# Attention scores as three single-pass products of split keys and queries, on row halves of the matmul array

## The chip, the cores and the metric

The kernel runs on one core of a Trainium2 chip. The core has a matmul engine (PE; its weight loads are listed apart as PEld), a vector engine (DVE), a scalar engine (ACT), a GpSimd engine (POOL) and DMA queues, all of which run their own instruction streams and wait for each other on semaphores. The metric is the device time of one execution in microseconds, median over runs; lower is better.

## What is computed

An attention layer with pooled queries feeds two feed-forward layers. Cut to what matters:

```python
q_pool = q.reshape(B, H, S // 2, 2, D).mean(axis=3)          # B=2, H=8, S=1152, D=64
scores = scale * np.matmul(q_pool, k.transpose(0, 1, 3, 2))  # 576 queries x 1152 keys for each of 16 heads
scores = scores - np.max(scores, axis=-1, keepdims=True)
attn = np.exp(scores)
attn = attn / (np.sum(attn, axis=-1, keepdims=True) + 1e-09)
x = np.matmul(attn, v)                                       # then heads are joined: 1152 tokens x 512
h = x @ w_in;  x = softplus(h) @ w_out                       # 512 -> 2048 -> 512
h = x @ w_in2; x = (P(h) / (Q(h) + 1e-6)) @ w_out2           # a rational function of h
```

q and k are drawn with a spread of 0.8, so the scores have to be accurate to well below one.

## The kernel before, in words

All work is described to a small planner (`Plan`): each operation has an engine, a duration that the author gives it, the buffers that it reads and writes, and a priority. `Plan.order` simulates the engines by these durations and writes the instruction streams in the order that it finds; the priorities are a start time by position in the work plus an offset from the tables `OFF` and `OFF2`. Buffers have no fixed addresses: each *kind* of buffer has a list of slots in SBUF (`arena`, `arena_r`) or in the eight PSUM banks, and a buffer takes a slot that is free. Kinds of phase 1 (the feed-forward layers) can share slots with kinds of phase 0 (the attention), and get them once those are all placed and done.

The attention runs over 16 heads, each in two *units* of 288 queries. For a head:

- keys and queries come in by DMA; POOL adds pairs of queries (L428);
- PE transposes the keys (L443, nine blocks of 128 keys, packed in pairs, so that the upper 64 rows of a packed block belong to one key block and the lower 64 to another) and the queries (L455). Each of the four transposed pieces of a head goes to PSUM bank 4 (kind `tp`, one slot, which it shares with `mT`) and is copied to SBUF: two pieces by ACT (L338), two by DVE (L340), chosen by `KEV` and `QEV`;
- for each unit, `scores` (L571) multiplies: keys are the stationary operand, queries move. A *pair* of key blocks is one operation; there are four of them in a unit, and the last has the ninth key block behind it, with its 288 queries divided over both row halves (144 each). The products are plain fp32 in four 64x64 tiles of the array. The result goes to one of two slots of two banks each (kind `sc`), where DVE takes the running maximum (L484) and ACT copies it to SBUF (L338);
- the maximum over keys goes through two PE transposes (L503, L513) and a DVE reduction (L507); DVE and POOL subtract it (L597), ACT takes the exponential (L604), PE multiplies with the values and with ones (L534);
- the row sums go through DRAM, POOL normalises (L631) and splits the result in a rounded part `xh` and a rest `xl` (L342, L353).

The feed-forward layers already compute with split operands: both factors are a part rounded to `float32r` and a rest, and three products (high-high, high-low, low-high) are summed (L721 for the first matrix, L803 for the second). `L353` is the line of the helper that subtracts, `L338` that of ACT copies, whatever the operation. The planner's cost of three such products with n columns is `pe_t(3, n)`; the costs of one scores operation were 0.476 us, and 0.724 us for the last of a unit.

## Time and profile before

| | us |
|---|---|
| median of 3 runs | 691.98 (691.31 to 693.44) |
| the profiled execution | 691.12 |
| its span in the trace | 689.3 |
| PE busy | 666.6 (97%) |
| DVE / ACT / POOL busy | 543.0 / 532.4 / 518.1 |

The times are of whole executions; the span is what lies between the first and the last instruction of the profiled one, so 1.8 us lie around it. Busy PE time is modelled: a matmul counts as busy until its result has drained, so the distance between the starts of two runs of matmuls is the better measure of their cost than their listed durations. In the trace, an fp32 product shows as two records, a `float32r` product as one.

### The profile page before, as it was taken

How to read it: one execution, taken by the hardware profiler on the slowest of the kernel's cores; microseconds unless marked ns; L12 is line 12 of the kernel's file. 1: busy time of each engine (PE TensorE's matmuls, PEld its weight loads, DVE VectorE, ACT ScalarE, POOL GpSimd, SP SyncE). 2: the span in 40 equal slices, each digit the busy share in tenths (PEclk: the TensorE clock that was granted, in tenths of full speed). 3: DMA queues.
4: the chain of work that ended last, by engine and by line, in shares of the span. 5: the costliest groups of instructions: out<-in, count | busy, mean ns of one | idle time of the engine just before them, and what ended most of it. 6: DMA issues, size and time to landing. Idle time of an engine off the chain costs nothing.

```text
span 689.3 us, 15479 instructions
## 1 busy us (share of the span) xinstructions
PE 666.6 (97%) x5892; PEld 507.6 (74%) x5892; DVE 543.0 (79%) x762; ACT 532.4 (77%) x1011; POOL 518.1 (75%) x513
## 2 busy tenths in 40 slices
PE   7899999999999999999999999999999999999997
PEld 4344444444444445699999999999988989888985
DVE  4788966677777799653447889999999997788896
ACT  4678877777777788768787977788877788976763
POOL 2456857465757576997778987899997799996773
PEclk9999999999999999999999999999999999999999
DMA  7233333222222333341033577898422022201011
GB/s 220 71 86 96 79 90 81 56 64 72 69 73 55 104 123 102 103 134 58 1 94 91 162 261 266 264 315 271 128 83 71 32 62 61 78 2 46 1 47 46
DMA packets 55546, 70.92 MB, mean 103 GB/s; under 512 B 11312, under 2 KB 36912, under 8 KB 55472
## 3 DMA queue, kind: packets, MB, share of 16 engines
q1 hardware_dynamic: 55472, 69.93, 33.2%
q8 instruction: 46, 0.75, 0.5%
q14 instruction: 28, 0.23, 0.1%
HBM read 58.99 MB, written 10.78 MB: 101 GB/s over the span
## 4 chain that ended last, share of the span: by engine, by line
PE 73%; DVE 8%; POOL 6%; ACT 5%; DMA 4%; issue 4%; SPq 0%; POOLq 0%; DVEq 0%; ACTq 0%
PE banks L721 25%; PE banks L803 25%; PE banks L534 11%; PE banks L571 7%; DVE arena L484 3%; ACT arena L338 3%; PE banks L503 1%; DVE banks L785 1%; DMA arena<-in_q_dram 1%; PE banks L443 1%; PE banks L513 1%; ACT arena L604 1%; DMA rr<-arena 1%; DVE arena L597 1%; PE banks L455 1%
## 5 line engine op out<-in xcount | busy, mean ns | idle before, releaser
L803 PE MATMUL banks<-arena_r 128*128 128x384 f32 (+1 forms) x1008 | 213.4, 359 | 1.4 <-DVE arena_r L353 0.8
L721 PE MATMUL banks<-xh,arena_r 128*128 128x384 f32 x768 | 211.5, 338 | 2.5 <-DVE arena_r L353 2.3
L803 PEld LDWEIGHTS banks<-arena_r 128*128 128x128 f32 x1008 | 181.4, 188 | 16.2 <-POOL arena_r L353 1.5
L338 ACT COPY arena<-banks 128x576 f32<-128x576 f32 (+5 forms) x293 | 140.0, 523 | 55.7 <-DVE arena L484 21.9
L721 PEld LDWEIGHTS banks<-xh,arena_r 128*128 128x128 f32 x768 | 140.4, 188 | 8.9 <-DVE arena_r L353 5.9
L721 PE MATMUL banks<-xl,arena_r 128*128 128x384 f32 x384 | 129.3, 337 | 0.0
L597 POOL TENSOR_TENSOR arena<-arena 128x1152 f32<-128x1152 f32 x32 | 85.2, 2663 | 56.8 <-ACT arena L338 56.2
L785 DVE RECIPROCAL banks<-arena 128x384 f32<-128x384 f32 x48 | 122.7, 2555 | 6.6 <-POOL arena L777 5.3
L484 DVE TENSOR_TENSOR arena<-banks,arena 128x576 f32<-128x576 f32 (+1 forms) x128 | 86.7, 679 | 37.1 <-ACT arena L338 18.7
L353 POOL TENSOR_TENSOR arena<-arena 128x384 f32<-128x384 f32 x96 | 97.4, 1020 | 12.5 <-ACT arena L755 8.4
L571 PE MATMUL banks<-arena 64*64 64x288 f32 (+1 forms) x1280 | 92.3, 396 | 6.4 <-DVE arena L484 4.4
L534 PE MATMUL banks<-arena 128*32 128x288 f32 (+1 forms) x1280 | 87.5, 387 | 1.2 <-ACT arena L604 0.8
L353 POOL TENSOR_TENSOR arena_r<-arena,arena_r 128x512 fp32r<-128x512 f32 x64 | 82.3, 1296 | 7.6 <-ACT arena_r L338 7.2
L604 ACT ACTIVATE arena<-arena 128x1440 f32<-128x1440 f32 (+1 forms) x64 | 82.8, 1293 | 6.6 <-POOL arena L597 3.3
L721 PEld LDWEIGHTS banks<-xl,arena_r 128*128 128x128 f32 x384 | 72.1, 188 | 1.3
L353 DVE TENSOR_TENSOR arena_r<-banks,arena_r 128x384 fp32r<-128x384 f32 x96 | 52.9, 551 | 24.7 <-ACT arena_r L338 24.3
L571 PEld LDWEIGHTS banks<-arena 64*64 64x64 f32 x1280 | 39.2, 133 | 42.0 <-ACT arena L338 11.6
L777 POOL TENSOR_TENSOR arena<-arena 128x384 f32<-128x384 f32 x48 | 49.0, 1020 | 22.5 <-ACT arena L771 22.3
L338 ACT CAST arena_r<-banks 128x384 fp32r<-128x384 f32 x96 | 45.9, 478 | 23.0 <-DVE banks L757 13.4
L771 ACT ACTIVATE arena<-banks,par 128x384 f32<-128x384 f32 x96 | 63.6, 684 | 0.0
L534 PEld LDWEIGHTS banks<-arena 128*32 128x32 f32 x1280 | 33.7, 109 | 35.1 <-issue 11.9
L757 DVE SCALAR_TENSOR_TENSOR banks<-banks,arena 128x384 f32<-128x384 f32 x48 | 27.1, 564 | 37.0 <-POOL arena L353 36.3
(55 smaller groups left out, 927.0 us busy)
## 6 DMA issues: line engine op xcount, KB each, us to landing
arena<-in_moe_w_in_dram SPq DMA_DIRECT2D x32, 512.0 KB
arena<-in_moe_w_out_dram SPq DMA_DIRECT2D x32, 512.0 KB
sp<-arena SPq DMA_DIRECT2D x32, 256.0 KB
arena<-sp SPq DMA_DIRECT2D x32, 256.0 KB
arena<-in_k_dram SPq DMA_DIRECT2D x16, 288.0 KB
arena<-in_q_dram SPq DMA_DIRECT2D x16, 288.0 KB
arena<-in_v_dram SPq DMA_DIRECT2D x16, 288.0 KB
arena<-rr SPq DMA_DIRECT2D x16, 144.0 KB
```

The costliest lines, as they stand in the source:

```text
L338: nc.scalar.copy(o, i)
L353: e.tensor_tensor(out=o, in0=a, in1=b, op=ALU.subtract)
L484: P.op("V", dve_t(m * HW), lambda: nc.vector.tensor_tensor(out=o(), in0=x(), in1=y(), op=ALU.max), r=r, w=w, at=t0 + (OFF['mx'] + 0.15 * j ...
L534: nc.tensor.matmul(out=out()[r:r + m, o:o + w], lhsT=lhs(x, y), rhs=st()[:, x, o:o + w], start=(c == 0 and first), stop=(c == KC - 1 and l ...
L571: nc.tensor.matmul(out=ps()[y:y + D, i, o:o + w], lhsT=kx()[D * i:D * i + D, x, y:y + D], rhs=qT()[D * i:D * i + D, q0:q0 + w], start=True ...
L597: (nc.vector, nc.gpsimd)[g].tensor_tensor(out=s, in0=s, in1=mB()[:, None, :].to_broadcast([128, n, HW]), op=ALU.subtract)
L604: nc.scalar.activation(out=s, in_=s, func=AF.Exp, scale=escale)
L721: nc.tensor.matmul(out=hp(), lhsT=w()[:, kk * 128:(kk + 1) * 128], rhs=x[:, kk, :], start=(kk == 0 and n == 0), stop=(kk == KD - 1 and n = ...
L771: return lambda: nc.scalar.activation(out=o(), in_=i(), func=AF.Identity, scale=sc, bias=bi)
L777: P.op("G", pool_t(CW), lambda: nc.gpsimd.tensor_tensor(out=Q(), in0=t(), in1=ah(), op=ALU.add), r=[t, ah], w=[Q], at=a("2q"))
L785: P.op("V", (69 + 6.25 * CW) / 1e3, lambda: nc.vector.reciprocal(out=h(), in_=Q()), r=[Q], w=[h], at=a("2r"))
L803: nc.tensor.matmul(out=o()[:, 0:w_], lhsT=lt, rhs=rh, start=(f == 0 and n == 0), stop=(f == FG - 1 and n == 2),)
```

## The change

Keys and queries are split like the operands of the feed-forward layers. Each of the four transposed pieces of a head is rounded to `float32r` by ACT (`kh`, `qh`), and DVE subtracts that from the piece in PSUM (`kl`, `ql`). A pair of key blocks is then three passes (high-high, high-low, low-high); in each pass two products with 64 rows and 128 columns of the array, one for each row half, replace the four 64x64 tiles. The ninth block stays behind the fourth pair. The planner's costs of a scores operation become 0.39 and 0.68 us, and it treats them as the same kind of matmul as those of the feed-forward layers (`mode=0`). The split parts live at the end of `arena_r`, where the eighth set of weight buffers and the buffers `gh` and `gl` of the feed-forward layers lie; room that becomes free in `arena` changes the slots there, with one `raw` buffer more outside the attention's slots. All offsets of the priorities are new.

```diff
 OFF = {
-    'wait': -8.882,
+    'wait': 28.77,
...
-KEV = "AV"
-QEV = "VA"
...
-    f1 = lay(0, arena, 0, LF, ("kr", 2, 2560), ("qr", 1, 3072), ("qm", 1, 3072), ("vf", 2, 2304), ("kx", 2, 2560))
+    f0 = lay(0, arena, 0, LF, ("kr", 2, 2560), ("qr", 1, 3072), ("qm", 1, 3072), ("vf", 2, 2304))
+    f1 = f0 + 4096
     f2 = lay(0, arena, f1, LF, ("s", 4, 10368))
-    f3 = lay(0, arena, f2, LF, ("q1", 2, 2304), ("mx", 2, 1152), ("ud", 2, 2304), ("sd", 2, 1152), ("uh", 2, 1152), ("rb", 1, 2304), ("xp", 1, 2304),
+    f3 = lay(0, arena, f2, LF, ("mx", 2, 1152), ("ud", 2, 2304), ("sd", 2, 1152), ("uh", 2, 1152), ("rb", 1, 2304), ("xp", 1, 2304),
              ("mp", 2, 2304), ("mb", 2, 1152), ("mc", 2, 32), ("dc", 2, 160), ("rc", 2, 64))
+    lay(0, arena_r, LR - 20480, LR, ("kh", 2, 2560), ("kl", 2, 2560), ("qh", 2, 2304), ("ql", 2, 2304))
...
     lay(1, arena_r, 0, LR, *wch * 8, *g * 4)
-    lay(1, arena, 0, f1, ("raw", 2, 4096), ("w23", 2, 2048), ("w2", 3, 2048))
+    lay(1, arena, 0, f0, ("raw", 1, 4096), ("w23", 2, 2048), ("w2", 3, 2048))
+    lay(1, arena, f0, f1, ("raw", 1, 4096))
...
-    lay(1, arena, f3, LF, ("raw", 1, 4096), ("w23", 1, 2048))
+    lay(1, arena, f3, LF, ("raw", 1, 4096), ("w23", 1, 2048), ("raw", 1, 4096))
...
-            kx = P.buf("kx", [128, KP, 128], F32)
-            qT = P.buf("q1", [128, SQ], F32)
+            kx = [P.buf(x, [128, KP, 128], F32R) for x in ("kh", "kl")]
+            qT = [P.buf(x, [128, SQ], F32R) for x in ("qh", "ql")]
             spare = ["mB", "pv", "sm"] if first else []
+
+            def halves(t, n, src, dst, key, at):
+                hi, lo = dst
+                P.op("A", act_t(n), lambda: cp("A", hi(), src()), r=[t], w=[key[0]], at=at)
+                P.op("V", dve_t(n), lambda: sub("V", lo(), src(), hi()), r=[t, key[0]], w=[key[1]], at=at)
...
-                ee = KEV[g]
-                P.op(ee, cp_t(ee, 128 * n, True), lambda: cp(ee, kx()[:, c0:c0 + n, :], t()[:, 0:n, :]),
-                     r=[t], w=[(kx, g)], at=t0 + OFF['tke'] * T)
+                halves(t, 128 * n, lambda: t()[:, 0:n, :], [lambda x=x: x()[:, c0:c0 + n, :] for x in kx],
+                       [(x, g) for x in kx], t0 + OFF['tke'] * T)
...
-                P.op(QEV[s], cp_t(QEV[s], HW, True), lambda: cp(
-                    QEV[s], qT()[:, s * HW:(s + 1) * HW].rearrange("p (j c) -> p j c", j=3), t()),
-                    r=[t], w=[(qT, s)], at=t0 + OFF['tqe'] * T)
+                halves(t, HW, t, [lambda x=x: x()[:, s * HW:(s + 1) * HW].rearrange("p (j c) -> p j c", j=3) for x in qT],
+                       [(x, s) for x in qT], t0 + OFF['tqe'] * T)
...
-                    for y in range(0, 128, D):
+                    for n, (a, y) in enumerate(((0, 0), (0, 1), (1, 0))):
                         for i in range(2):
                             q0 = hf * HW + i * step
                             nc.tensor.matmul(
-                                out=ps()[y:y + D, i, o:o + w],
-                                lhsT=kx()[D * i:D * i + D, x, y:y + D],
-                                rhs=qT()[D * i:D * i + D, q0:q0 + w],
-                                start=True,
-                                stop=True,
+                                out=ps()[:, i, o:o + w],
+                                lhsT=kx[a]()[D * i:D * i + D, x, :],
+                                rhs=qT[y]()[D * i:D * i + D, q0:q0 + w],
+                                start=(n == 0),
+                                stop=(n == 2),
                                 skip_group_check=True,
                             )
 
-            P.op("P", 0.724 if last else 0.476, mm, r=[(qT, hf), (kx, 0), (kx, 1)] if j > 1 else [(qT, hf), (kx, 0)],
-                 w=[ps], at=at, mode=4)
+            P.op("P", 0.68 if last else 0.39, mm, r=[(x, hf) for x in qT] + [(x, g) for x in kx for g in range(1 + (j > 1))],
+                 w=[ps], at=at, mode=0)
```

## Rows read from the trace of the kernel before

**Rows 1.** Page, part 1: busy time, share of the span, instructions.
```profile
PE 666.6 (97%) x5892; PEld 507.6 (74%) x5892; DVE 543.0 (79%) x762; ACT 532.4 (77%) x1011; POOL 518.1 (75%) x513
```

**Rows 2.** Busy time by stage: window, length, each engine's busy us, PEclk, DMA, GB/s.
```profile
19.00:22.20 3.20, 0.61 (x7) 0.43 (x7) 3.08 (x4) 1.21 (x5) 2.09 (x2) 1.00 0.00 0
22.20:26.00 3.80, 3.80 (x25) 1.54 (x29) 1.19 (x4) 2.90 (x4) 2.35 (x1) 0.55 0.31 83
...
173.62:189.87 16.25, 15.82 (x236) 7.67 (x239) 11.97 (x20) 12.72 (x22) 11.48 (x12) 1.00 0.26 71
189.87:206.11 16.24, 15.81 (x235) 7.65 (x239) 11.95 (x20) 12.54 (x22) 9.11 (x8) 1.00 0.22 62
...
302.00:500.00 198.00, 197.05 (x1124) 195.84 (x1123) 149.93 (x238) 158.03 (x340) 171.82 (x188) 1.00 0.54 173
```

**Rows 3.** Chain of work that ended last, 176 to 189 us: start, us, what.
```profile
175.86 0.25 PE banks L455 x3
176.10 1.38 PE banks L571 x24
...
183.84 0.77 DVE arena L484
184.61 0.04 issue
184.65 0.72 PE banks L571 x8
...
188.28 1.13 PE banks L571 x16
```

**Rows 4.** Timeline of PE, start, us, instructions, idle time before them.
```profile
184.65 0.72 PE L571 MATMUL banks<-arena 64*64 64x288 f32 x8 [0.38 <-DVE arena L484]
```

**Rows 5.** Timeline of PE where feed-forward matmuls follow the attention's.
```profile
264.29 0.96 PE L571 MATMUL banks<-arena 64*64 64x288 f32 x16
...
266.20 0.45 PE L721 MATMUL banks<-xh,arena_r 128*128 128x384 f32 x1
266.48 0.34 PE L721 MATMUL banks<-xl,arena_r 128*128 128x384 f32 x1
...
288.30 0.79 PE L803 MATMUL banks<-arena_r 128*128 128x384 f32 x3
```

**Rows 6.** Chain, dense stretches of 384 columns (L721) and of 512 (L803).
```profile
343.27 4.17 PE banks L721 x24
...
526.52 3.40 PE banks L803 x15
```

**Rows 7.** Timeline of PE, narrow windows: the ninth block's matmuls and the ones behind.
```profile
192.81 0.42 PE L571 MATMUL banks<-arena 64*64 64x144 f32 x8
...
193.06 0.66 PE L571 MATMUL banks<-arena 64*64 64x288 f32 x8
```

**Rows 8.** Timeline of PE, the opening transposes, whose operands are float32r.
```profile
1.62 4.43 PE L653 MATMUL banks<-identr 128*128 128x128 f32 x36 [1.62 <-DVE ones L867]
5.88 0.74 PE L443 MATMUL banks<-ident,arena 128*128 128x128 f32 x5
```

**Rows 9.** Groups by shape, ACT and DVE: busy us, mean ns, idle before.
```profile
L338 ACT COPY arena<-banks 128x288 f32<-128x288 f32 x80 | 31.7, 406 | 18.1 <-PE banks L513 9.6 <-DVE arena L484 5.1 <-DVE arena L597 2.2
...
L353 DVE TENSOR_TENSOR arena_r<-banks,arena_r 128x384 fp32r<-128x384 f32 x96 | 52.9, 551 | 24.7 <-ACT arena_r L338 24.3
...
L484 DVE TENSOR_TENSOR arena<-banks,arena 128x288 f32<-128x288 f32 x32 | 14.6, 456 | 0.9
...
L340 DVE COPY arena<-banks 128x288 f32<-128x288 f32 x16 | 7.1, 445 | 1.3 <-PE banks L455 1.2
L340 DVE COPY arena<-banks 128x256 f32<-128x256 f32 x16 | 6.7, 420 | 1.9 <-PE banks L443 1.9
```

**Rows 10.** Timeline, all engines: how long pieces stand in bank 4.
```profile
175.69 0.41 PE L455 MATMUL banks<-ident,arena 96*128 96x96 f32 x3
...
176.33 0.44 DVE L340 COPY arena<-banks 128x288 f32<-128x288 f32 x1
...
177.65 0.47 PE L455 MATMUL banks<-ident,arena 96*128 96x96 f32 x3
...
179.15 0.31 PEld L443 LDWEIGHTS banks<-ident,arena 128*128 128x128 f32 x3 [0.47 <-ACT arena L338]
```

**Rows 11.** Timeline of POOL: the fifteenth of sixteen weight rests of the first layer's group.
```profile
302.71 1.31 POOL L353 TENSOR_TENSOR arena_r<-arena,arena_r 128x512 fp32r<-128x512 f32 x1
```

More of the change, by code (lines that the diff above doesn't have):

```diff
@@ L202 @@
 OFF = {
-    'wait': -8.882,
-    'slack': -1.382,
-    'ld': -812.521,
-    'tk': -11.818,
-    'tke': 1536.06,
-    'sq': -727.689,
-    'tq': -10.601,
-    'tqe': -306.514,
-    'lv': 7144.53,
-    'sc': 81.048,
-    'ev': 1752.92,
-    'mx': 906.024,
-    'mt': -1814.3,
-    'mr': 522.686,
-    'mb': -625,
-    'sh': 8796.51,
-    'ex': -150.754,
-    'stick': 770.627,
-    'ms': -5296.43,
-    'shg': -186.538,
-    'exg': 7835.02,
-    'sm': 1013.29,
-    'so': -57.276,
-    'pv': 808.435,
-    'pvs': -103.047,
-    'po': -726.257,
-    'nm': 456.872,
+    'wait': 28.77,
+    'slack': -13.759,
+    'ld': 0.198,
+    'tk': -16.966,
+    'tke': -4195.19,
+    'sq': 375.411,
+    'tq': -15.761,
+    'tqe': -260.576,
+    'lv': -1665.22,
+    'sc': 27.543,
+    'ev': 608.597,
+    'mx': 419.752,
+    'mt': -1241.4,
+    'mr': -207.398,
+    'mb': -4279.26,
+    'sh': 3841,
+    'ex': 1779.84,
+    'stick': 3184.49,
+    'ms': -2890.58,
+    'shg': -16.114,
+    'exg': 1464.57,
+    'sm': 3221.9,
+    'so': 379.479,
+    'pv': 1651.99,
+    'pvs': -414.881,
+    'po': 1120.04,
+    'nm': 315.914,
 }
 OFF2 = {
-    'ld': -118.557,
-    'hi': -1626.93,
-    'lo': 751.869,
-    'sp': -617.197,
-    'ld2': 1471.26,
-    '1a': 823.014,
-    '1d': 391.426,
-    '1y': -4944.66,
-    '1r': -1591.47,
-    '1z': -190.564,
-    '1g': 362.064,
-    'gh': 7560.96,
-    'gl': -160.245,
-    '2h': 193.884,
-    '2a': 314.78,
-    '2t': 100.782,
-    '2q': 2434.09,
-    '2b': 877.088,
-    '2A': 7670.04,
-    '2m': 2938.22,
-    '2n': -108.014,
-    '2r': 2130.37,
-    '2g': -602.386,
-    'out': 2838.23,
-    'end': 10454.9,
-    'c1': -1510.66,
-    'c2': -5603.53,
-    'co': 18.915,
-    's0': 517.435,
-    's1': 2446.21,
+    'ld': 590.296,
+    'hi': 384.693,
+    'lo': -1389.58,
+    'sp': 848.971,
+    'ld2': 286.76,
+    '1a': 587.131,
+    '1d': 1539.75,
+    '1y': -4596.15,
+    '1r': -788.05,
+    '1z': -652.263,
+    '1g': -441.645,
+    'gh': 28.699,
+    'gl': -1205.75,
+    '2h': -1678,
+    '2a': -475.889,
+    '2t': -298.715,
+    '2q': -4211.42,
+    '2b': 21.98,
+    '2A': 3258.02,
+    '2m': 1597.4,
+    '2n': 626.472,
+    '2r': 854.862,
+    '2g': -511.212,
+    'out': 5907.98,
+    'end': 4845.89,
+    'c1': -4112.39,
+    'c2': -1549.96,
+    'co': 16.991,
+    's0': 1668.77,
+    's1': 200.585,
 }
```

## The prediction

> **What bounds the kernel now.** I read the share of busy time first, then the busy time by stage, then the chain of work inside one head. PE is busy 97% of the span and no other engine passes 79% [rows 1], but that is a mean over two stages. In the feed-forward stage PE has 197.05 of 198.00 us [rows 2]: nothing there can pay but fewer matmul columns, and this change takes none. In the attention the trace repeats: from about 40 us to 265 us one head (two units) takes 16.24 us, and in two such windows PE is busy 15.8 us, ACT 12.5 to 12.7, DVE 12.0, POOL 9.1 to 11.5 [rows 2]. The chain in a head runs through PE's own order nearly everywhere. The one place where it leaves PE is a wait of 0.38 us for a scores slot that DVE's maximum still reads [rows 3, 4]. So the attention is bound by PE too, with 0.4 us of 16.24 lost to others. What PE saves in a head comes off the end as long as ACT and DVE, which the change loads, keep up.
>
> **The scores before.** A run of two pairs of key blocks takes 1.13 us; a run of two pairs and the ninth block takes 1.38 us [rows 3]. The ninth block is the difference, 0.25 us; the narrow windows agree, with its eight records between 192.81 and 193.06 [rows 7]. The planner's 0.476 a pair and 0.248 for the ninth leave 0.17 to 0.18 us for entering such a run. A unit is 4 x 0.48 + 0.24 = 2.16 us and a head 4.32, plus four entries of 0.17 us.
>
> **The scores after.** One pass is two products, one for each row half. That the halves run side by side is seen today: a pair is eight records of 288 columns in 0.48 us, 60 ns each, where a single-pass product at 2.4 GHz would stream 288 columns in 120, and the two row halves write the same partitions in different banks, as they will. For the length of a pass I take the feed-forward matmuls: 24 with 384 columns in 4.17 us, 174 ns; 15 with 512 in 3.40 us, 227 ns [rows 6]. That is 0.41 ns a column, so 288 columns take 174 - 96 x 0.41 = 135 ns. The lower bound is bare streaming, 120 ns. Three passes are 0.405 us (0.36 at least) for a pair.
>
> The ninth block has 144 columns a pass, 60 ns of streaming and 75 with the 15 ns that the rows above leave over; but each pass loads two sets of 128 weight columns. No row shows such a load alone, so it is bounded by its neighbours. The ninth block today loads 64 columns for each of its records, at 31 ns a record [rows 7], so 62 ns for 128 columns and 124 a pass, still under the 135 of a full pass. A query transpose loads 128 columns and moves 96 in 0.25 / 3 = 83 ns [rows 3]: 166 a pass. The float32r transposes at the start take (5.88 - 1.62) / 36 = 118 ns with load and stream [rows 8]: 236 a pass. The first is the nearest, because there too loads for different tiles alternate; the others hold a load and a stream that may not overlap. So the ninth costs 3 x 75 to 3 x 124, 0.23 to 0.37 us; I take 0.29, the middle. It is also what the diff's planner costs imply (0.68 - 0.39), and the old costs in that table match the trace (0.248 against 0.25).
>
> A unit is then 4 x 0.405 + 0.29 = 1.91 us, 0.25 less; a head saves 0.50. Entering a float32r run costs 0.28 - 0.17 = 0.11 us where a feed-forward run follows the attention [rows 5], against 0.17: four entries save 0.06 each, 0.25 a head. Together 0.75 us a head. Of 225 us in which PE is the bound there are 225 / 16.24 = 13.9 heads: **10.5 us off**.
>
> The Trainium skill, TensorEngine Tiling (Array Packing), Key Properties, has it that a change of tiling mode drains the engine. Row halves beside whole-array matmuls would be such a change, and the 0.25 us of entries would be gone: 7.0 us instead of 10.5. No run here shows the entry to row halves.
>
> **What is added.** In a head two pieces that DVE copied go to ACT, 288 columns at 406 ns and 256 at some 380: ACT +0.79 us. DVE loses copies of 445 and 420 ns and gains four subtractions from PSUM, 551 ns for 384 columns, 456 for each 288, some 430 for 256 [rows 9]: 1.89 - 0.87 = +1.03 us. At a head of 15.5 us ACT stands at 13.5 (87%, from 78) and DVE at 13.0 (84%, from 74). Both stay under PE. But both are in order, and behind each added instruction stand the copies and maxima that free the scores slots, for which PE already waits 0.38 us a head. From nothing to twice that 0.38 may come on top; I take 0.15 us a head, 2.1 us. In the first head one subtraction and a handover (0.46 + 0.2 us, by the same rows) lie before the first scores: 0.6 us.
>
> Bank 4 is held longer. A query piece is there from 175.69 to 176.77 and the next from 177.65 to 179.15, the last copied by ACT, with the key transposes waiting behind [rows 10]. The six holds of a head (four pieces and two maxima) are some 7 us by such rows. Each piece now waits for ACT and then DVE, so about 0.7 us more: 10 of 15.5 us. That is hidden, since pieces are made a head ahead, until waits add over 5 us.
>
> The new place of the split parts costs nothing. They end with the last scores (264.29 + 0.96 us), the first matmul that needs `gh` starts at 288.30 [rows 5], and the eighth weight set is made from 302.71 on [rows 11]. If the attention's end moved there late by 20 us it would cost; it moves earlier. The extra `raw` slot and the new offsets move work that is off the path. What they do to the few bubbles of the feed-forward stage (about 1 us each) I count as 0 with 2 us either way.
>
> **Sum.** 691.1 - 10.5 + 2.1 + 0.6 = 683.3 us for the profiled execution. The median stands 0.9 above it: **684 us**.
>
> **Rivals.**
> *The loads are the bound (slower).* A pass waits for two weight loads instead of for columns. At 83 ns a load each of the 15 passes of a unit is 166 ns, a unit 2.49 us, 0.33 more than now; 32 units give 10.6 us, less 3.5 of entries: 699 us. At 118 ns a unit is 3.54: 692 + 32 x 1.38 - 3.5 = 733 us. It decides from a pass of (2.16 + 0.12) / 15 = 152 ns, 76 ns a load. For it speaks that every row with 128 weight columns and few moving ones is above 76; against it that those rows have one tile, and the ninth block's 64 columns pass in 31.
> The Trainium skill, TensorE: Matmul & The Clock Gate, LDWEIGHTS, gives columns / 1.2 ns for a load, and so speaks against this change: an estimate by it is 107 ns a load, 214 a pass, a unit of 3.2 us and 692 + 32 x 1.05 - 3.5 = 722 us. The trace does not bear this out for loads in tiles, since 64 columns would be 53 ns there, and are 31 [rows 7].
> *ACT, DVE or bank 4 take PE's place (no change).* The saving turns into waits before the scores and key transposes: if 0.75 us a head is lost so, the head stays at 16.24 us and the time at 692. For it: DVE already ends PE's only wait. Against: both keep 2 us free a head.
> *The halves don't overlap (not what it says).* Six products of 135 ns are 0.81 us a pair, and six of 75 ns for the ninth are 0.45; a unit 3.69 us, 692 + 32 x 1.53 = 741 us. The four tiles of today speak against it.
>
> **How the numbers follow.** Forecast 0.66, loads 0.15 (most of it near 699), no change 0.12, halves 0.03, and 0.04 for a new order that is worse at several places at once, near 697. Within 0.3% (about what a measurement of this kernel can tell from no change) is 689.9 to 694.1. Faster 0.66, same 0.12, slower 0.22. The forecast's own range is 675 (passes at 120 ns and 75 for the ninth save another 0.2 us a unit, no added waits) to 690. To leave out no more than 2 in 10 the range reaches to 699.
>
> PE's clock adds a little: after the 2.6 us in which PE stands idle before 22.2 us the granted clock is 0.55 on average to 26 us [rows 2], some 1.7 us lost; a start with another gap may have that or not, and the range holds it.
>
> **What would show it.** Right: a run of two pairs near 0.81 us plus an entry of 0.1, the ninth near 0.29, a head near 15.6 us with PE still busy over 96% of it, the feed-forward stage as long as before. Wrong: a pass over 150 ns with weight loads back to back; or short passes with PE idle behind L338, L353 or L484 for over half a microsecond a head; or the head as forecast and the start or the handover to the feed-forward stage longer by several microseconds.

## The result, and the profile after

| | before | after |
|---|---|---|
| median, us | 690.15 (689.22 to 693.44, 9 runs) | 695.83 (692.88 to 696.74, 9 runs) |
| the profiled execution / its span | 691.12 / 689.3 | 695.97 / 694.2 |

After over before is 1.0068, 95% interval 1.0049 to 1.0088: the changed kernel is 0.7% slower. The forecast was 684 and "faster"; the time lies in the range (675 to 699), the direction was wrong.

The lines of the changed kernel that matter: L575 scores, L488 running maximum, L507 and L517 the maximum's transposes, L511 its reduction, L601 shift, L608 exponential, L538 values, L336 ACT's copies and roundings, L351 subtractions, L683, L686 and L689 the three DVE instructions of a weight conversion, L725 and L807 the feed-forward matrices. Each experiment below has its own numbering, a few lines off.

The page's busy times, then busy time by stage (window, length, busy us and instructions of PE, PEld, DVE, ACT, POOL, PEclk, DMA share, GB/s), against [rows 1] and [rows 2]:

```profile
PE 662.9 (95%) x5572; PEld 548.5 (79%) x5572; DVE 561.9 (81%) x794; ACT 551.2 (79%) x1043; POOL 519.8 (75%) x513
```
```profile
10.40:17.00 6.60, 5.84 (x35) 4.42 (x35) 4.84 (x9) 2.96 (x6) 0.12 (x1) 0.50 0.96 262
17.00:30.90 13.90, 12.55 (x74) 8.71 (x74) 9.55 (x16) 9.60 (x17) 7.34 (x4) 0.50 0.24 67
148.76:164.53 15.77, 15.15 (x212) 9.63 (x212) 12.79 (x21) 13.56 (x24) 9.14 (x8) 1.00 0.25 70
264.30:269.26 4.96, 0.00 (x0) 0.00 (x1) 4.78 (x9) 2.27 (x6) 4.62 (x7) 0.71 0.63 191
302.00:500.00 198.00, 196.09 (x1113) 193.74 (x1112) 148.70 (x239) 159.90 (x335) 171.02 (x186) 1.00 0.57 177
```

Three things are to be seen. The head shrank from 16.24 to 15.77 us. PE's granted clock stands at 0.50 (1.2 GHz, its lower level) for 20.5 us of the start, where before it was low for about 4 us [rows 2]; it fell behind an idle time of PE of 1.5 us, in which PE waits for keys (to 8.97). And a stretch of 5 us near the end of the attention has no matmul at all, while DVE and POOL are full. Where the 4.9 us went is read from the starts of the same work in both traces:

| start of | before | after | difference |
|---|---|---|---|
| first scores | 8.57 | 10.57 | +2.0 |
| values of unit 0 | 25.83 | 29.44 | +3.6 |
| values of unit 4 | 62.02 | 61.49 | -0.5 |
| values of unit 16 | 161.80 | 156.42 | -5.4 |
| values of unit 28 | 258.11 | 251.48 | -6.6 |
| values of unit 29 | 265.57 | 277.03 | **+11.5** |
| ninth feed-forward tile | 305.10 | 311.73 | +6.6 |
| last matmul | 685.07 | 689.94 | +4.9 |

Two neighbouring units, 28 and 29, turn a lead of 6.6 us into a lag of 11.5. Some of that comes back at once, because PE does feed-forward tiles meanwhile; 13 us are gone by the ninth tile. PE's timeline there (start, us, instructions, idle time before and what ended it), where [rows 5] has the same place of before; first, from before, the values of units 28 and 29:

```profile
258.11 1.18 PE L534 MATMUL banks<-arena 128*32 128x288 f32 x16 [0.52 <-ACT arena L604]
...
265.57 0.69 PE L534 MATMUL banks<-arena 128*32 128x288 f32 x8
```
```profile
251.48 0.69 PE L538 MATMUL banks<-arena 128*32 128x288 f32 x8
...
261.72 0.34 PE L725 MATMUL banks<-xh,arena_r 128*128 128x384 f32 x1
269.26 0.88 PE L507 MATMUL banks<-ident,arena 128*96 128x128 f32 x3 [7.20 <-DVE arena L689]
269.79 2.27 PE L807 MATMUL banks<-arena_r 128*128 128x384 f32 x6
271.85 0.52 PE L725 MATMUL banks<-xh,arena_r 128*128 128x384 f32 x1
...
277.03 2.39 PE L538 MATMUL banks<-arena 128*32 128x288 f32 x40
...
283.00 0.45 PE L725 MATMUL banks<-xh,arena_r 128*128 128x384 f32 x1 [1.94 <-DVE arena_r L351]
```

And what DVE did meanwhile, from its timeline:

```profile
261.90 0.46 DVE L488 TENSOR_TENSOR arena<-banks,arena 128x288 f32<-128x288 f32 x1
262.28 0.68 DVE L683 TENSOR_SCALAR banks<-arena 128x512 int32<-128x512 int32 x1
263.00 0.70 DVE L686 SCALAR_TENSOR_TENSOR banks<-arena,banks 128x512 int32<-128x512 int32 x1
263.73 0.69 DVE L689 SCALAR_TENSOR_TENSOR arena<-arena,banks 128x512 int32<-128x512 int32 x1
...
268.53 0.68 DVE L689 SCALAR_TENSOR_TENSOR arena<-arena,banks 128x512 int32<-128x512 int32 x1
```

Between a unit's last maximum (261.90) and the transposes that need it (269.26) DVE makes three weight conversions, 9 x 0.70 = 6.3 us. Their buffer `cv` lies in bank 4, where L507 has to write, so PE waits for the last L689. PE's clock adds to the loss. Behind each of the two waits of the timeline it stands at 0.50 (the columns are as above):

```profile
269.26:273.20 3.94, 3.94 (x15) 3.82 (x16) 3.46 (x5) 1.48 (x2) 3.86 (x5) 0.50 0.51 159
283.46:286.87 3.41, 3.41 (x15) 2.97 (x18) 2.87 (x5) 3.21 (x5) 3.24 (x5) 0.50 0.43 120
```

The first six matmuls there, of 384 columns, start over 2.06 us (269.79 to 271.85), 0.34 us each, where [rows 6] have 0.174. An estimate from these rows: half of 3.94 + 3.41 us is 3.7, and with the waits of 7.2 and 1.9 us that makes 12.8 of the 13 us.

The last instructions of the sixteen conversions of the first layer start before at 11.2, 30.7, 44.1, 59.0, 70.1, 79.7, and then from 243.2 on; after at 12.3, and then all others from 256.5 on. On DVE's timeline the sixth and seventh of before, then the first and second of after:

```profile
79.67 0.67 DVE L685 SCALAR_TENSOR_TENSOR arena<-arena,banks 128x512 int32<-128x512 int32 x1
243.16 0.67 DVE L685 SCALAR_TENSOR_TENSOR arena<-arena,banks 128x512 int32<-128x512 int32 x1
```
```profile
12.35 0.69 DVE L689 SCALAR_TENSOR_TENSOR arena<-arena,banks 128x512 int32<-128x512 int32 x1
256.49 0.68 DVE L689 SCALAR_TENSOR_TENSOR arena<-arena,banks 128x512 int32<-128x512 int32 x1
```

**Five conversions that lay in the first heads now lie at the attention's end.** That is a reading of two traces; the experiments test it, and the price of the new form beside it. Nor is all of the lead a saving of the new form. Of the 6.6 us at unit 28, 4.7 are won from unit 2 to unit 12, where the changed kernel makes no conversion: before needs 83.6 us for these five heads (from 14.0 to 18.8 us each, and 16.24 only behind them), after 78.8. The conversions are not all of that: with four of them held back, in a run below, before takes 82.2.

### The profile page after: what moved, and what is told of

Its sections match the earlier page's. It is cut to its first block, busy times and chain, and to the rows that moved or that the text cites. A ratio compares the mean times of both kernels' runs of the same rounds, so it can differ in the third digit from the quotient of the medians.

```text
span 694.2 us, 14921 instructions
## 1 busy us (share of the span) xinstructions
PE 662.9 (95%) x5572; PEld 548.5 (79%) x5572; DVE 561.9 (81%) x794; ACT 551.2 (79%) x1043; POOL 519.8 (75%) x513
## 4 chain that ended last, share of the span: by engine, by line
PE 73%; DVE 11%; ACT 8%; DMA 3%; issue 2%; POOL 2%; SPq 0%; DVEq 0%; POOLq 0%; ACTq 0%
PE banks L725 25%; PE banks L807 24%; PE banks L538 10%; PE banks L575 8%; DVE arena L601 4%; ACT arena L336 4%; ACT arena L608 2%; DVE arena L488 2%; PE banks L507 2%; DVE banks L789 2%; PE banks L449 1%; DMA arena<-in_q_dram 1%; DVE arena_r L351 1%; PE banks L517 1%; DMA arena<-sp 1%
## 5 line engine op out<-in xcount | busy, mean ns | idle before, releaser
L725 PE MATMUL banks<-xh,arena_r 128*128 128x384 f32 x768 | 214.1, 341 | 5.0 <-DVE arena_r L351 4.3
L807 PE MATMUL banks<-arena_r 128*128 128x384 f32 (+1 forms) x1008 | 214.5, 360 | 0.0
L807 PEld LDWEIGHTS banks<-arena_r 128*128 128x128 f32 x1008 | 182.6, 189 | 13.8
L336 ACT COPY arena<-banks 128x576 f32<-128x576 f32 (+5 forms) x261 | 131.3, 531 | 38.2 <-DVE arena L488 14.3
L725 PEld LDWEIGHTS banks<-xh,arena_r 128*128 128x128 f32 x768 | 141.6, 189 | 11.6 <-DVE arena_r L351 8.8
L601 POOL TENSOR_TENSOR arena<-arena 128x1152 f32<-128x1152 f32 x32 | 85.3, 2665 | 73.4 <-ACT arena L336 73.4
L725 PE MATMUL banks<-xl,arena_r 128*128 128x384 f32 x384 | 130.2, 339 | 0.2 <-POOL xl L351 0.2
L351 DVE TENSOR_TENSOR arena_r<-banks,arena_r 128x384 fp32r<-128x384 f32 (+2 forms) x160 | 82.7, 517 | 47.8 <-ACT arena_r L336 46.5
L351 POOL TENSOR_TENSOR arena<-arena 128x384 f32<-128x384 f32 x96 | 97.8, 1021 | 15.7 <-ACT arena L759 10.0
L488 DVE TENSOR_TENSOR arena<-banks,arena 128x576 f32<-128x576 f32 (+1 forms) x128 | 86.5, 677 | 28.2 <-ACT arena L336 20.8
L336 ACT CAST arena_r<-banks 128x384 fp32r<-128x384 f32 (+2 forms) x160 | 72.6, 454 | 26.3 <-DVE banks L790 9.9
L538 PE MATMUL banks<-arena 128*32 128x288 f32 (+1 forms) x1280 | 83.1, 388 | 8.0 <-ACT arena L608 8.0
L575 PE MATMUL banks<-arena_r 64*128 64x288 f32 (+1 forms) x960 | 88.6, 320 | 1.9 <-ACT arena L336 0.7
L608 ACT ACTIVATE arena<-arena 128x1440 f32<-128x1440 f32 (+1 forms) x64 | 82.7, 1292 | 5.1 <-DVE arena L601 5.0
L351 POOL TENSOR_TENSOR arena_r<-arena,arena_r 128x512 fp32r<-128x512 f32 x64 | 82.6, 1299 | 4.6 <-ACT arena_r L336 4.5
L575 PEld LDWEIGHTS banks<-arena_r 64*128 64x128 f32 x960 | 69.3, 196 | 17.5 <-issue 6.2
L725 PEld LDWEIGHTS banks<-xl,arena_r 128*128 128x128 f32 x384 | 72.7, 189 | 1.6 <-POOL xl L351 0.5
L538 PEld LDWEIGHTS banks<-arena 128*32 128x32 f32 x1280 | 35.4, 109 | 40.8 <-ACT arena L608 11.0
L775 ACT ACTIVATE arena<-banks,par 128x384 f32<-128x384 f32 x96 | 61.8, 687 | 0.0
L601 DVE TENSOR_TENSOR arena<-arena,banks 128x1440 f32<-128x1440 f32 x32 | 52.7, 1646 | 1.6 <-ACT arena L336 1.0
```

The lines of the kernel that those rows point to most:

```text
L336: nc.scalar.copy(o, i)
L351: e.tensor_tensor(out=o, in0=a, in1=b, op=ALU.subtract)
L488: P.op("V", dve_t(m * HW), lambda: nc.vector.tensor_tensor(out=o(), in0=x(), in1=y(), op=ALU.max), r=r, w=w, at=t0 + (OFF['mx'] + 0.15 * j ...
L538: nc.tensor.matmul(out=out()[r:r + m, o:o + w], lhsT=lhs(x, y), rhs=st()[:, x, o:o + w], start=(c == 0 and first), stop=(c == KC - 1 and l ...
L575: nc.tensor.matmul(out=ps()[:, i, o:o + w], lhsT=kx[a]()[D * i:D * i + D, x, :], rhs=qT[y]()[D * i:D * i + D, q0:q0 + w], start=(n == 0), ...
L601: (nc.vector, nc.gpsimd)[g].tensor_tensor(out=s, in0=s, in1=mB()[:, None, :].to_broadcast([128, n, HW]), op=ALU.subtract)
```

## Experiments: the price of the new form

**The form alone, in the order of before.** Keys and queries are rounded by the copies of before; each pair is three passes on row halves, all of the rounded parts, so the rests are left out of the scores. The rounded parts lie at the end of `arena_r`. Nothing is added on ACT or DVE, and the order of all engines is that of before.

```diff
-                    for y in range(0, 128, D):
+                    for _ in range(3):
...
-                                out=ps()[y:y + D, i, o:o + w],
-                                lhsT=kx()[D * i:D * i + D, x, y:y + D],
+                                out=ps()[:, i, o:o + w],
+                                lhsT=kx()[D * i:D * i + D, x, :],
```

> The kernel before, its order and its copies unchanged, only the scores in the new form: keys and queries are rounded by the copies that there are, and a pair of key blocks is three passes on the two row halves, all three of the rounded parts (each overwrites the one before, so that the rests are left out and PE's work is that of the changed kernel). This measures the price of the form alone, without the added ACT and DVE work and without a new order. The prediction's price (0.75 us a head): head 15.5, total 679 to 682. Theory now (weight loads show at the start of each operation, the form is worth 0.13 to 0.28 us a head): head 15.95 to 16.1, total 686 to 689. Rival (loads the bound): head at or above 16.24, 690 or more.

Measured: 688.10 us (683.59 to 689.74) against 689.85, ratio 0.9959 (0.9935 to 0.9984). The figure goes with the clock: eight of the ten executions have a granted clock of 0.987 to 0.992 over their span and take 687.45 us or more, and two have 0.997 and take 683.59 and 683.84. The profiled one, 688.38, has 0.990. Busy time by stage at the start and in two heads:

```profile
18.00:30.90 12.90, 10.90 (x73) 7.67 (x69) 7.15 (x12) 7.05 (x11) 4.41 (x2) 0.52 0.17 48
170.65:186.58 15.93, 15.44 (x216) 9.22 (x212) 11.96 (x19) 12.73 (x22) 11.47 (x11) 1.00 0.25 70
186.58:202.51 15.93, 15.44 (x215) 9.22 (x211) 11.95 (x19) 12.73 (x22) 9.16 (x7) 1.00 0.25 70
```

The form is worth 16.24 - 15.93 = 0.31 us a head, not 0.75. PE's timeline shows where the rest stays, two pairs alone and two with the ninth block:

```profile
172.83 1.06 PE L572 MATMUL banks<-arena_r 64*128 64x288 f32 x12
173.82 0.53 PE L504 MATMUL banks<-ident,arena 128*96 128x128 f32 x3
...
176.76 1.39 PE L572 MATMUL banks<-arena_r 64*128 64x288 f32 x18
178.09 0.31 PE L535 MATMUL banks<-arena,ones 128*2 128x72 f32 x8
```

A run of two pairs goes from 172.83 to 173.82, 0.99 us where the prediction had 0.81 and an entry of 0.11; with the ninth it is 1.33, where it had 1.21. The single records of these runs tell why. The two halves of a pass start 2 to 9 ns apart, and passes follow each other every 0.130 us, as forecast (0.135). But the first pass of a run starts at 172.828 and the second at 173.067, 0.24 us later. The first weight load starts at 172.826 and the second at 172.934, and the first pass's records are 0.399 us long, the next ones' some 0.29: so one load of 0.108 us shows at the start of a run, and the stream of 0.13 comes on top. From the last pass to the next work it is another 0.22. So 6 x 0.13 = 0.78 us of passes make a run of 0.99. In the run with the ninth block its three passes take 0.067, 0.113 and 0.111 us, the last two the distance of their loads, and the full pass behind them 0.18 instead of 0.13: 0.34 us in all, 1.33 - 0.99.

**The changed kernel with the old products**, in its own order: four fp32 tiles of 64x64 read the rounded parts.

```diff
-                    for n, (a, y) in enumerate(((0, 0), (0, 1), (1, 0))):
+                    for y in range(0, 128, D):
...
-                                lhsT=kx[a]()[D * i:D * i + D, x, :],
+                                lhsT=kx[0]().bitcast(F32)[D * i:D * i + D, x, y:y + D],
...
```

> The changed kernel with its scores multiplied as before, in plain fp32 on four 64x64 tiles, from the rounded parts alone; splits, buffers and the order of every instruction stream are those of the changed kernel, so that only the form of the scores differs (the rests are computed and not used). The prediction's price of the form, 0.75 us a head: a steady head grows from 15.77 to 16.5 us. The price read from the two traces, 4.96 against 5.24 us of PE a head without waits: it grows by 0.3 us or less, to 15.8 to 16.1, because some of it falls into PE's wait of 0.62 us a head. Rival (the head's length is set by DVE and ACT): it stays at 15.77 within 0.05.

Measured: 695.93 us, one run, within the 692.88 to 696.74 of the changed kernel. Over ten heads (units 4 to 24) it loses 1.3 us, 0.13 a head; it had won 2.0 by unit 4. The clock is low for 6.8 us at the start, not for 20.5:

```profile
8.90:15.70 6.80, 6.05 (x41) 3.00 (x45) 5.02 (x9) 2.79 (x6) 0.00 (x0) 0.50 0.96 289
15.70:31.00 15.30, 11.44 (x141) 5.44 (x137) 11.57 (x19) 11.28 (x21) 7.46 (x4) 1.00 0.25 78
```

So of the 0.47 us by which the changed kernel's heads are shorter, 0.13 is the form's in this order. By type of work, values take 7.11 us a head instead of 7.58 (from the starts of PE's timeline), being issued in four runs instead of seven: that is the new order, since the run with the old products, in the same order, has 7.11 too.

**The changed kernel without the third pass** (the product of the keys' rests is left out; order kept).

```diff
-for n, (a, y) in enumerate(((0, 0), (0, 1), (1, 0))):
+for n, (a, y) in enumerate(((0, 0), (0, 1))):
...
-                                stop=(n == 2),
+                                stop=(n == 1),
```

> The changed kernel without the third pass of its scores (rest of the keys times rounded queries is left out); order kept. A pass is 0.13 us of a pair and 0.11 of the ninth block when loads are hidden, so PE has 2 x (4 x 0.13 + 0.11) = 1.26 us a head less to do. If PE bounds the head it shrinks from 15.77 to 14.5 us. If the chain from scores over DVE's maximum and shift and ACT's exponential to the values bounds it (PE waits 0.62 us a head there), it shrinks by what lies on that chain alone, one to two passes for each unit: 0.3 to 0.6 us, to 15.2 to 15.5, and PE's waits grow by the rest.

Measured: 686.77 us, one run. Of 1.26 us of passes a head gives back 0.5 (15.25 us), and PE's wait before the values grows from 0.62 to some 0.75 us. The chain of work in a head of the changed kernel shows what stands there (start, us, what):

```profile
158.06 0.90 PE banks L575 x12
...
159.04 0.76 DVE arena L488
...
159.82 1.67 DVE arena L601
...
162.09 0.66 ACT arena L336
...
163.17 1.31 ACT arena L608
164.48 0.04 issue
164.53 1.18 PE banks L538 x16
```

Behind the last scores lie a maximum, a shift, copies and an exponential, 5.5 us in which PE has other work for all but 0.62. Before, PE's wait was 0.38 [rows 4].

**The changed kernel without the rests' subtractions** from the third head on (the passes read old rests).

```diff
-lambda: sub("V", lo(), src(), hi()),
+(lambda: sub("V", lo(), src(), hi())) if hd < 2 else (lambda: None),
```

> The changed kernel, its order kept, without the subtractions that make the rests of keys and queries from the third head on (the passes read old rests instead): DVE has 1.9 us less to do in a head, and bank 4 comes free after ACT's rounding. Theory (a head is set by one chain of DVE's last maximum, its shift, ACT's copies and exponential, in which the subtractions have no place): the head stays within 0.1 us of 15.77, 694 to 697. Rival (the added DVE work and the longer hold of bank 4 are what keeps the head from 15.5): the head falls to 15.5 or less, 690 to 692.

Measured: 694.16 us, one run; a head is 15.55 us. That is between the two forecasts, and a single run: by it the subtractions cost 0.22 us a head, though the chain names none of them. That they stand in DVE's queue ahead of the maxima would explain it, which no run shows.

**One pass in the order of before**: scores of rounded keys and queries alone, the rests left out.

```diff
-                    for _ in range(3):
+                    for _ in range(1):
```

> The same with one pass instead of three: scores of rounded keys and queries alone, a less accurate product than either kernel's. PE has (8 x 0.26 + 2 x 0.21) = 2.5 us a head less to do. Theory (behind PE stands a chain of DVE and ACT that is nearly as long as the head; two passes instead of three gave 0.47 of 1.26 us): head 15.2 to 15.6, total 676 to 684. Rival (PE alone sets the head): head below 14, total below 662.

Measured: 679.56 us (678.38 to 680.00), ratio 0.9833 (0.9803 to 0.9863): faster than both kernels, with a less accurate product. A head is 14.89 us, shorter than expected (15.2 to 15.6) but far from what PE's 2.5 us less would make:

```profile
177.62:192.51 14.89, 13.30 (x175) 6.71 (x171) 11.86 (x19) 12.73 (x22) 9.16 (x7) 1.00 0.29 75
```
```profile
175.23 0.47 PE L572 MATMUL banks<-arena_r 64*128 64x288 f32 x4 [0.39 <-ACT arena L338]
176.56 0.40 PE L572 MATMUL banks<-arena_r 64*128 64x288 f32 x2 [0.87 <-DVE arena L485]
```

PE now waits 1.26 us a head for scores slots that ACT and DVE still read. The attention's end keeps its order, and the lead of 10.6 us at unit 28 reaches the end (12.7 at the last matmul).

## Experiments: the start

**Weight loads later**: the early weight loads but the first are held until the second head's row sums are written, since the changed kernel issues three of them from 4.09 to 5.12 us, when the loads of the first heads are issued but not all landed, and before only one (3.14).

```diff
-r=[] if l == 0 and F < 3 else [("rr", GATE)]
+r=[] if l == 0 and F == 0 and io == 0 else [("rr", 1)] if l == 0 and F < 3 else [("rr", GATE)]
```

> The changed kernel, with the two spare weight loads that it issues at 4.6 and 5.1 us (and the next at 13.1) held until the second head is normalised; the rest of the order is the same, the weights are used from 256 us on. Theory (start lost to loads): the first key and query loads share the DMA engines with these, PE stands idle between 6.5 and 11.8 us, its granted clock falls to 0.5 at 10.4 us and stays there to 30.9. With the loads held the first scores start 1 to 2 us earlier than 10.57, the clock stays up longer, and the whole is 2 to 5 us shorter than the changed kernel. Rival (the start is late because value loads go first and because the rounded and rest parts add steps): first scores within 0.5 us of 10.57, clock as before, time within 1 us of the changed kernel.

Measured: 696.60 us (695.06 to 697.20), ratio 1.0091 (1.0073 to 1.0109) to before. The first values come 1.2 us earlier, the first scores 0.6 (10.01), and the clock is low for the same 20.5 us. The loads are a small part of the late start. What no run changes is the order of the first loads: after issues two value loads first (0.74) and its keys at 1.63, before its keys at 0.74 and the values at 3.61.

**Longer warm-up**: 20 more transposes before the keys arrive, so that PE doesn't stand idle until 9.0 us.

```diff
-            for _ in range(NWARM):
+            for _ in range(NWARM + 20):
```

> The changed kernel, its order kept, with 20 more warm-up transposes (56 instead of 36, 0.13 us each, 2.7 us) so that PE has no idle time of 1.5 us before the keys' second piece arrives at 9.0 us. Theory (the start is late because PE's clock falls after that idle time and the row-half passes then run at half speed for 20 us): the granted clock stays at 1.0 past 10 us, the first values come 2 to 4 us earlier than 29.4, and the total is 2 to 4 us less than the changed kernel's, 692 to 694. Rival (the start waits for data, for ACT's rounding and DVE's subtractions; the clock costs little): first values at 28.5 or later, total 695 to 697.

Measured: 696.81 us (695.82 to 701.97), ratio 1.0105 (1.0059 to 1.0151); first values at 29.19. The theory fell, and the figures are the rival's: PE was busy for 2.73 of the 3 us to 9.0 and the clock at 0.97 in the next 3, but it was at 0.50 from 12 to 30 all the same. The idle time had only moved: in those next 3 us PE was busy for 0.99. So this run doesn't tell whether a full clock would bring the values forward. One execution speaks against a gain in the total: of the changed kernel's nine, it has a granted clock of 0.992 over its span, against 0.977 to 0.980 in the others, and takes 695.85 us, where their median is 695.83. The runs above show when the clock is low: with the order of before and only the form changed to about 31 us, with the old form in the new order to 15.7.

## Experiments: the attention's end

**Conversions spread**: in the changed kernel four of the late conversions are put into early heads, every other instruction keeps its place (their buffer lies in SBUF; some weights come out wrong, while the amount of work is the same).

```diff
+            for i, o in enumerate((v1, v2, v3)):
+                o.start = vs[3 * (n - 1) + i].start - 1e-3
...
-        for o in P.order(0.01 * OFF['slack'], 0.01 * OFF['wait'], OFF['stick']):
+        for o in spread(P.order(0.01 * OFF['slack'], 0.01 * OFF['wait'], OFF['stick'])):
```

> The changed kernel, with four of the five weight conversions that it does between 256 and 274 us (conversion 1 to 4; three DVE operations, one ACT cast, one POOL subtraction each) done one operation per unit between heads 2 and 8, in place in SBUF instead of bank 4, their loads with them; every other operation keeps its place. Theory (handover lost to DVE): the 7.2 us in which PE waits at 262 us for a maximum queued on DVE behind three conversions shrink to under 2 us, the granted clock doesn't fall there, and the kernel is 7 to 12 us shorter than the changed one, that is 684 to 689 us, also below the kernel before. Each unit with an inserted operation may cost up to 0.3 us, 4 us in all, so the gain can be 4 us smaller. Rival (the handover is slow because ACT and DVE lag with the attention's own work, now that scores come faster): PE still waits over 5 us for the last maximum, and the time is within 2 us of the changed kernel.

Measured: 697.97 us (697.06 to 698.77), ratio 1.0114 (1.0095 to 1.0132). Neither the 684 to 689 of the theory nor the wait of the rival came. The last instructions of the four now start at 45.0, 71.4, 94.9 and 120.1 us, and cost 2.2 us there (the values of unit 16 start at 158.62, not 156.42). PE transposes the last maximum at 264.43 now, but a gap stayed behind it; PE's timeline, then DVE's:

```profile
271.16 2.56 PE L810 MATMUL banks<-arena_r 128*128 128x384 f32 x6 [6.20 <-ACT arena_r L338]
```
```profile
270.03 0.56 DVE L764 SCALAR_TENSOR_TENSOR banks<-banks,arena 128x384 f32<-128x384 f32 x1 [5.65 <-POOL arena L353]
```

PE's order had been made for late weights: one tile of the first matrix, then its second matrix, which waits for the softplus chain through ACT, POOL and DVE. Nothing else was queued in front, and the last unit's reduction stood behind that chain on DVE. Taking the conversions out of an order made around them gave nothing back, so this run alone doesn't decide between the conversions and the order.

**Before with late conversions**: four of the six early conversions of the kernel before are held to the end; the planner orders the rest.

```diff
-r=[] if l == 0 and F < 3 else [("rr", GATE)]
+r=[] if l == 0 and F < 1 else [("rr", GATE)]
```

> The kernel before, with four of its six early weight conversions (the third to the sixth) held until near the end of the attention, by one condition on their loads; the planner orders the rest anew. Theory (the attention's end is bound by DVE work that has lost its place earlier): 4 x 3 instructions of 0.70 us = 8.4 us of DVE move in front of or among the last units' maxima, PE waits several us there behind them, and the time is 6 to 12 us above the kernel before, 697 to 702, with the steady heads unchanged at 16.2 us. Rival (DVE has time left at 79% busy, so conversions can run anywhere): within 2 us of the kernel before.

Measured: 704.68 us (704.34 to 705.61), ratio 1.0206 (1.0172 to 1.0240), 13.7 us slower. About 3 us are lost in the first heads, whose order also changed; the steady heads are as before (the lag is 3.0 at unit 16 and 2.8 at unit 28). The lag is 2.8 at the first feed-forward tile and 15.0 at the ninth. PE's longest wait there ends with POOL, which subtracts for the weights' rests (from 310.0 us, in that wait, to 316.8 the granted clock is 0.50):

```profile
305.67 2.01 PE L803 MATMUL banks<-arena_r 128*128 128x384 f32 x10 [0.66 <-POOL arena_r L353]
311.78 1.01 PE L721 MATMUL banks<-xh,arena_r 128*128 128x384 f32 x2 [3.76 <-POOL arena_r L353]
```

So late conversions cost about as much (12.2 us, from a lag of 2.8 to one of 15.0) in a kernel that has none of the change's other parts, though the order that the planner finds around them is new here too. The expectation had the sign, a size somewhat too small (6 to 12 us) and the wrong place: not the last units' maxima waited here, but the tiles, for weights.

**Attention first**: the changed kernel with all operations of the attention ranked ahead of the feed-forward layers.

```diff
-M0 = -225.024
+M0 = 30000.0
```

> The changed kernel with every operation of the attention ranked ahead of every one of the feed-forward layers (one constant). Theory (the same DVE work has to fit in before the eighth tile, whatever comes first): the last units lose their hole of 7.2 us and finish about 10 us earlier, but the feed-forward tiles then wait for weights, and the total is no better than 2 us under the changed kernel: 694 to 704. Rival (the order alone is at fault: work of the feed-forward stage was put in front of the last units): the 7.2 and 1.9 us of waiting vanish and nothing takes their place, 686 to 689.

Measured: 704.48 us (702.40 to 705.12), ratio 1.0195 (1.0163 to 1.0228), half a microsecond above the top of the theory. The values of unit 29 start at 260.19 instead of 277.03, so the hole is gone; and the ninth tile starts at 322.83 instead of 311.73. The wait moved:

```profile
301.45 1.01 PE L725 MATMUL banks<-xh,arena_r 128*128 128x384 f32 x2 [4.94 <-POOL arena_r L351]
```

With the conversions late, putting the attention first is worse by 8.7 us. Other orders were not tried, so this doesn't show that the changed kernel's is the best.

**Fewer conversions**: five of the sixteen are left out of the changed kernel (the first set's weights stand in), the loads of the others held two heads later, and the order computed anew.

```diff
+            if 1 <= 2 * F + io <= 5:
+                W[0, F, io] = W[0, 0, 0]
+                return
...
-GATE = 11
+GATE = 13
```

> The changed kernel without five of its sixteen weight conversions (the second to the sixth: their loads, 15 instructions of DVE, five each of ACT and POOL; the tiles use the first set's weights in their place), the loads of the others held two heads later, and the order computed anew. It leaves out as much conversion work as the kernel before does early, in the shade of its first heads. Theory (that work, come late, is what eats the gain): 15 x 0.70 = 10.5 us of DVE vanish from the attention's end, the wait of 7.2 us with them, and the 6 to 7 us that the heads save reach the end: 684 to 689. Rival (the hole is of the new order or of the split parts' place, whatever is converted): 693 to 697.

Measured: 689.67 us (688.71 to 691.90), ratio 0.9987 (0.9966 to 1.0009) to before, 6.2 us under the changed kernel, 0.7 above what was expected. The values of unit 29 start at 265.26, level with before, and the hole of 7.2 us is closed. But one long wait stays, and again it is POOL's:

```profile
306.36 0.87 PE L728 MATMUL banks<-xh,arena_r 128*128 128x384 f32 x2 [3.60 <-POOL arena_r L351]
```

Without the five conversions, and in the new order that goes with it, about half of the 13 us is back. It comes late: at the ninth tile (309.59) this run is 2.1 us ahead of the changed kernel, at the 21st 7.2. The other eleven, whose loads were held longer here, still keep POOL behind. How much of the rest belongs to that later loading and how much to the order of the changed kernel isn't separated.

Why the changed kernel's planner puts no conversion into its heads stays open. Bank 4, which a conversion needs for 2.1 us, is held longer there, by each piece until ACT and then DVE have read it. But the new offsets also rank the conversions otherwise. By the diff `c1` goes from -1510.66 to -4112.39 (in steps of 3.95 us, counted off from `M0`) and `mx` from 906.024 to 419.752 (in steps of 7.4 us), and of what can start the smaller rank goes first: conversions at 5742 stood ahead of maxima at 6704, and at 16019 they stand behind maxima at 3106. No run tries the one without the other.

## Why the prediction was wrong, point by point

- **"PE is the bound of a head, 0.4 us of 16.24 lost to others": half right.** PE was busy throughout, yet a chain through DVE and ACT is close behind. Two passes instead of three gave 0.5 of 1.26 us, one pass in the order of before 1.35 (16.24 to 14.89) of some 2.8, which is 2.5 for the two passes and 0.31 for the form. And the head of 16.24 us doesn't hold from 40 us on: the five heads from unit 2 to unit 12 take 16.7 on average.
- **"0.75 us a head from the scores": the term was mis-sized.** A pass was right (0.13, forecast 0.135), the ninth block's own passes too (0.067 + 0.113 + 0.111 = 0.29, forecast 0.29), though the pass behind them takes 0.05 more. The entries were wrong. I took 0.11 us for entering a run, less than the 0.17 of the fp32 tiles, from feed-forward matmuls [rows 5]; measured it is 0.99 - 0.78 = 0.21, because a weight load of 0.108 us shows at the start of the run. So the 0.25 us a head of entries are gone, as in the prediction's 7.0 us; whether a drain has a part in that no run shows. The form is worth 0.31 us a head in the order of before and 0.13 in the new one.
- **"At 31 ns for 64 columns": a misreading of [rows 7].** Those records belong to four tiles, which load side by side: in the trace of before the four loads start 6 to 7 ns apart (192.812 to 192.831) and the next four 0.12 us behind the first. They say nothing of one load. The Trainium skill, TensorE: Matmul & The Clock Gate, LDWEIGHTS, has columns / 1.2, 107 ns for 128 columns. I set that aside; the traces of the new form agree with it (0.108 to 0.109 us from a first load to the next). The Trainium skill, TensorEngine Tiling (Array Packing), Key Properties, says that tiles load weights in parallel, and the loads of the two halves start 3 to 4 ns apart. Read together the two sections give an estimate of 3 x 107 ns = 0.32 us for the ninth block, against 0.34 measured, and they would have warned me off the 31 ns. The estimate by the first section beside the rival "loads the bound" had the right price for a load and the wrong sum, since it counted two loads one behind the other.
- **"0.15 us a head for ACT and DVE": about right.** The subtractions cost 0.22, by one run; no run takes out ACT's added copies.
- **"First head 0.6 us": wrong in size, and nearly without effect.** First values came 3.6 us late, but at unit 4 the changed kernel was level. The new form itself costs about 2 us there: the run with the old products is 2.0 us ahead of the changed kernel at unit 4, and the run with the new form in the order of before is 2.1 us behind that kernel at unit 10; in both pairs the granted clock at the start differs.
- **"The extra `raw` slot and the new offsets ... 0 with 2 us either way": the step that failed.** By unit 28 the lead was 6.6 us, somewhat less than the 7.8 of the forecast (10.5 less 2.1 and 0.6), and for other reasons. The 13 us lost behind it were in no term: five conversions moved from the heads to the handover, where PE waited 7.2 and 1.9 us. Whether "bank 4's longer hold is hidden" failed with it is open. The prediction looked for trouble at the handover in the new place of the split parts and in `gh`, and not in the conversions of the early heads, which cost little there (2.2 us for four, by the run that spread them). The rival with a worse order (697, chance 0.04) had the time and the sign; its mechanism was not spelled out. The list of signs did name this one, a handover longer by several microseconds. That the time lies in the range is luck: the range reached 699 for the rival of the loads, which did not come.
- **"Feed-forward stage as long as before": right**, 1.7 us shorter from the ninth tile to the end.

The sum after the fact: 691.1 - 6.6 (to unit 28, the start's loss included) + 13.2 (to the ninth tile) - 1.7 = 696.0 us, the profiled execution (695.97).

## What to carry to other kernels

Work of a later stage that a kernel does early, where it costs little, is part of every price (here four conversions cost 2.2 us in the heads of one kernel, and holding four to the end of the other cost 13.7): ask of each change whether that work still finds its place, and list where it lies before trusting a saving per iteration. Short runs of matmuls pay for a weight load at their start (0.108 us here) that a long run hides, so price them from short runs. And an order computed for one set of costs is one piece: in the run that spread the conversions and kept the order, the wait only went to the next in line.

## What the runs showed of the hardware that was not expected

- With passes on row halves PE's granted clock stayed at its lower level longer. In the order of before, with PE's work alone changed, it was 0.52 on average from 18.0 to 30.9 us; in before it was low only behind 22.2 us, for about 4 us [rows 2]. The changed kernel had 0.50 for 20.5 us, and the 64x64 tiles in the same order 0.50 for 6.8 us. In the steady heads shown above it was 1.00. It isn't so in every execution: one of nine of the changed kernel and two of ten of the form in the order of before have a clearly higher granted clock over their span (0.992 and 0.997).
- At the start of a run two loads of 128 weight columns for the two row halves start 3 to 4 ns apart, and the next two 0.108 to 0.109 us later (172.826 to 172.938 us, and 176.761 to 176.873).
